# One launch of masked attention and a gated product: the second chunk's attention steps moved to later slots of the first product stage

## The chip, the cores and the metric

The kernel runs as one program on one core of a Trainium2 chip. The metric is the device time of one execution, in microseconds (us); it is the median of several runs. The profile is one more execution of the same program, taken with the hardware profiler. TensorE is called PE below, VectorE DVE, ScalarE ACT, GpSimd POOL, and SyncE, which issues most loads, SP.

## What is computed

Attention over 4 batches, 8 heads, 768 positions, head size 64, in which a query sees the first 4 keys (sinks) and the last 128 keys. Its output is the input of a gated product with weights of 512 x 1536, 512 x 1536 and 1536 x 512:

```python
scores = scale * q @ k.T
scores = np.where(is_sink | in_window, scores, -1e9)
a = np.exp(scores - scores.max(-1, keepdims=True))
x = (a / (a.sum(-1, keepdims=True) + 1e-09)) @ v      # (4*768, 512) after joining the heads
return ((x @ w_a) * (x @ w_b)) @ w_out                # (3072, 512)
```

The weights come to the chip as 64-bit floating numbers, two 32-bit words each, and are made into 32-bit ones there.

## The kernel before

The 3072 rows are worked off in 8 chunks of 2 to 4 blocks of 128 rows. Chunk 0 has 4 blocks (512 rows, batch 0), chunk 1 has 2 (the rest of batch 0). Each chunk has an attention phase, which gives its `xf`, and a product stage, `moe`. While the product stage of chunk c runs, the attention of chunk c+1 is worked in between. The attention of chunk 0 stands alone ahead of everything (`first_attention`, tiles `kp`, `qp`, `p`, `t`, `avp`, `sktp`, `skp`).

**Product stage.** Twelve values of j. For each, `half("a", j)` and `half("b", j)` make 12 matmuls of 512 columns each (L852): each of x and the weight is held as a high part and a remainder (`xh`, `xl`; `wh`, `wl` inside one tile `w`), and of the four products the three larger are added. ACT copies a to `g` (L871), DVE multiplies it by b (L877), ACT rounds it to `gh` (L880), DVE makes the remainder `gl` (L882). Then `project` of the j before multiplies with the third weight into `o`, another 12 matmuls (L861). So one j is 36 matmuls of 512 columns. In chunk 0, PE works this off in the order a, b, o of the j before.

**Weights.** They are made during chunk 0 alone, a pair of two weights at a time: DVE shifts and joins words (L335, L337), ACT scales the low words (L336), DVE adds (L344), ACT rounds to the high part (L349), DVE takes the remainder (L354). `ahead` calls `weights_to` ahead of each third of a j, and pins these instructions to program order. The loads, `raw`, are issued by SP.

**Attention of the next chunk.** The generator `pipeline` is advanced by `between(s)`, called three times in a j, at slots s = 0, 1, 2, ... 35. Its first step is `do_prep` of head 0, which issues the loads of k, q, v (`kr`, `qr`, `v`, `vsr`) and makes high parts (`round`, L381, in chunk 1 on ACT) and remainders (`rest`, L386, in chunk 1 on DVE). Each later step makes the scores of one block of one head (two matmuls `s`, L493), the masking on DVE (L501), exp on ACT (L503), and so on to `p`; two steps later its transposes (`t`, L539), and after every second head a product with v (L434, in chunk 1 into the tile `t`). All this has one PSUM tile for scores and one for the rest in chunk 1. How many steps are to be taken by slot s is the variable `want`.

A scheduler orders the instructions of each engine; it may put an instruction ahead of earlier ones of the program if it is ready, but not those that are given to `keep_in_program_order`, which keep their order among themselves. Every engine works its list off in order. PE's list has each matmul with its weight load (PEld).

The functions that the diff touches, and what calls them:

Of the kernel before, what the change touches and what calls it, by code (L numbers as in the profile page):

```python
# [7 lines left out]
F32 = mybir.dt.float32  # L8
# [5 lines left out]
ALU = mybir.AluOpType  # L14
# [22 lines left out]
SINGLE, PAIRS = 2, 14  # L37
WARM = 8
FILL = {1: 3, 2: 6, 3: 2, 4: 2, 5: 2, 6: 2}
HALF, QUIET, MID = 4, 6, 18  # L40
H_MIN = 1.375 * 2.0 ** -12
H_SUM = 65536.0
I_SIGN = -2147483648
# [14 lines left out]
def verdict(tc, cp, ident, chk, val, gp):  # L58

    nc, pin = tc.nc, tc.keep_in_program_order  # L60
    V = nc.vector
    bad = cp.tile([P, 8], F32, name="bad")
    mm = cp.tile([P, 2], F32, name="mm")
    V.tensor_reduce(mm[:, 0:1], chk[:, :6 * NJ], axis=AX.X, op=ALU.min)
    V.tensor_reduce(mm[:, 1:2], chk[:, 6 * NJ:], axis=AX.X, op=ALU.max)
    pin(V.tensor_scalar(bad[:, 0:1], mm[:, 0:1], H_MIN, None, op0=ALU.is_ge))
    pin(V.tensor_scalar(bad[:, 1:2], mm[:, 1:2], H_SUM, None, op0=ALU.is_lt))
    pin(V.tensor_scalar(bad[:, 2:3], val[:, 0:1], 0.0, None, op0=ALU.is_ge))
    pin(V.tensor_scalar(bad[:, 3:4], val[:, 0:1], float(NS), None, op0=ALU.is_le))
    pin(V.tensor_scalar(bad[:, 4:5], val[:, 1:2], 1.0, None, op0=ALU.is_ge))  # L70
    pin(V.tensor_scalar(bad[:, 5:6], val[:, 1:2], float(P), None, op0=ALU.is_le))
    good = cp.tile([P, 2], F32, name="good")
    V.tensor_reduce(good[:, 0:1], bad[:, 0:6], axis=AX.X, op=ALU.min)
    flag = cp.tile([1, 1], I32, name="flag")
    nc.tensor.transpose(gp, good[:, 0:1], ident)
    V.tensor_reduce(flag, gp, axis=AX.X, op=ALU.min)
    return nc.values_load(flag[0:1, 0:1], min_val=0, max_val=1,
                          skip_runtime_bounds_check_because="a comparison gives 0 or 1")
# [139 lines left out]
class Fast:  # L218
# [159 lines left out]

    def round(self, o, i):
        if self.no_gpsimd:  # L380
            self.nc.scalar.copy(o, i)  # L381
        else:
            self.nc.gpsimd.tensor_scalar(o, i, 1.0, 1.0, op0=ALU.mult, op1=ALU.mult)  # L383

    def rest(self, o, i, high):
        (self.nc.vector if self.no_gpsimd else self.nc.gpsimd).tensor_tensor(o, i, high.bitcast(F32), op=ALU.subtract)  # L386

    def halves(self, h):
        return (slice(0, D), slice(D, P)) if h % 2 == 0 else (slice(D, P), slice(0, D))
# [509 lines left out]
    def run(self, scalars, verdict):  # L899
        chunks = CHUNKS  # L900

        order = self.order = sorted(((k, j) for j in range(NJ) for k in "abo"), key=lambda w: 3 * w[1] + (0, 1, 5)["abo".index(w[0])])
        done, loaded = [0], [0]

        def weights_to(n, ahead):
            wide = range(SINGLE, 2 * PAIRS)
            while loaded[0] < min(n + ahead, len(order)):
                if loaded[0] >= len(order) - 4 and done[0] <= 2 * PAIRS:
                    break
                self.load_weight(loaded[0])  # L910
                loaded[0] += 1
            while done[0] < min(n + DELAY, len(order) + DELAY):
                k = done[0]
                done[0] += 1
                singles = lambda d: 0 <= k - d < len(order) and k - d not in wide
                if singles(3):
                    self.weight_low(k - 3, 1)
                if k % 2 == 0 and k - 2 in wide:
                    self.weight_low(k - 2, 2)
                if singles(2):  # L920
                    self.weight_high(k - 2, 1)
                if singles(1):
                    self.weight_sum(k - 1, 1)
                if k % 2 == 1 and k - 1 in wide:
                    self.weight_sum(k - 1, 2)
                    self.weight_high(k - 1, 2)
                if singles(0):
                    self.weight_bits(k, 1)
                if k % 2 == 0 and k in wide:
                    self.weight_bits(k, 2)  # L930

        light = [c for c in range(2, len(chunks) - 1) if chunks[c + 1][1] == 0]
        checks = [(c, 3 * j) for c in light for j in range(2, 11)]
        checks += [(len(chunks) - 1, 3 * j + i) for j in range(9) for i in range(2)]

        b, t0, nt = chunks[0]

        x = self.wp.tile([P, NK, nt * P], F32, tag=f"w{3 * NJ // 2 - 1}", name="xf0")
        xf = [x[:, i, :] for i in range(NK)]
        first = self.first_attention(b, nt, xf)  # L940
        next(first)
        val = scalars()
        self.masks(val)
        self.val = val
        self.verdict = lambda gp: verdict(val, gp)
        for k, _ in enumerate(first, 1):
            if k >= STEP0 and (k - STEP0) % 3 < 2:
                weights_to(done[0] + 1 - DELAY, 4 + DELAY)
        for c, (b, t0, nt) in enumerate(chunks):
            gen = None  # L950
            if c + 1 < len(chunks):
                nb, nt0, nnt = chunks[c + 1]
                nxf = self.new_xf(c + 1)

                self.banks = ("t", "o2") if nt == 2 else ("t",)
                if c == 1:
                    self.join_masks()
                gen = (self.attention if c else self.attention_in_one_bank)(nb, nt0, nnt, nxf)
                steps = H * nnt + 6
            taken = [0]  # L960

            def between(s):
                if gen is None:
                    return
                if c:
                    want = min(steps, -(-steps * (s + 1) // (3 * NJ - 3)))
                else:
                    n = HALF * nnt + 1
                    want = max(-(-n * (s + 1 - QUIET) // (MID - QUIET)), 1)
                    if s >= MID:  # L970
                        want = min(steps, n - (n - steps) * (s + 1 - MID) // (3 * NJ - 3 - MID))
                while taken[0] < want:
                    next(gen, None)
                    taken[0] += 1

            def ahead(s):
                weights_to(max(s + AHEAD, done[0] + 1 - DELAY), LOADS)
                if (c, s) in checks:
                    self.check_weight(*order[checks.index((c, s))])
                elif self.unchecked:  # L980
                    self.check_weight(None, 0)

            self.moe(b * S + t0 * P, nt, xf, between, ahead, c + 1 == len(chunks), c > 1)
            if gen is not None:
                for _ in gen:
                    pass
                xf = nxf
        return val, self.ok
# [73 lines left out]
```

## Time and profile before

| what | value |
|---|---|
| median of 3 runs | 771.61 us (770.12 to 772.09) |
| the profiled execution's own time | 771.76 us |
| its span from first to last instruction | 770.0 us |
| granted TensorE clock over the span | 0.994 |
| PE busy | 755.8 us (98%) |
| DVE busy | 407.1 us (53%) |
| ACT busy | 417.1 us (54%) |
| POOL busy | 239.9 us (31%) |

The profile's page gives shares over the whole span, and the span cut in 40 slices of 19.25 us, each digit the busy share of its slice in tenths. The attention of chunk 0 fills about the first 38 us, the product stage of chunk 0 runs from 37.95 to 165 us, and seven more product stages follow. A timeline row has start, duration, engine, line, operation and tiles; in brackets the idle time of that engine just before it, and what ended it. Since matmuls overlap, the time from one start to the next, not the duration, is what one costs PE.

### The profile page before, as it was taken

The page shows a single profiled execution, that of the slowest core. Times are in us where ns is not written, and L with a number is a line of the kernel's source. Part 1 is how long each engine was busy: PE and PEld are TensorE (multiplying, and loading weights), DVE is VectorE, ACT ScalarE, POOL GpSimd, SP SyncE. Part 2 cuts the span into 40 slices and gives each one's busy share as a digit, 9 for nine tenths or more (in the row PEclk, how much of TensorE's full clock was granted, in tenths as well). Part 3 has the DMA queues.
Part 4 walks back from the last instruction along what each step waited for, and adds up shares of the span by engine and source line. Part 5 has one row for each costly group of instructions (what it writes and reads, how often), then busy time and mean ns, then how long its engine had stood idle before and what let it go on. Part 6 is the DMA issues. An engine that isn't in the chain of part 4 may idle for free.

```text
span 770.0 us, 13053 instructions
## 1 busy us (share of the span) xinstructions
PE 755.8 (98%) x4335; PEld 659.3 (86%) x4336; DVE 407.1 (53%) x1435; ACT 417.1 (54%) x1252; POOL 239.9 (31%) x305
## 2 busy tenths in 40 slices
PE   9989999999999999999999999999999999999996
PEld 4548777789889998999999999999998999899996
DVE  6997999956644454354433454244543445333221
ACT  5865877746645565365434554355664545434431
POOL 1100000155514544165531544224533544102110
PEclk9989999999999999999999999999999999999999
DMA  8995101231221442311211211113333112015511
GB/s 279 333 381 191 39 15 56 73 125 55 59 72 44 122 143 88 114 36 47 63 56 52 60 42 32 63 54 104 111 107 114 65 51 67 2 51 185 170 47 44
DMA packets 43272, 73.35 MB, mean 95 GB/s; under 512 B 4480, under 2 KB 23744, under 8 KB 43200
## 3 DMA queue, kind: packets, MB, share of 16 engines
q1 hardware_dynamic: 40144, 66.96, 26.9%
q10 hardware_dynamic: 3024, 5.51, 1.9%
q8 instruction: 35, 0.57, 0.3%
q14 instruction: 37, 0.30, 0.1%
q0 software_dynamic: 32, 0.00, 0.0%
HBM read 66.16 MB, written 6.29 MB: 94 GB/s over the span
## 4 chain that ended last, share of the span: by engine, by line
PE 88%; DVE 6%; ACT 3%; DMA 1%; issue 1%; SPq 0%; ACTq 0%; DVEq 0%; POOLq 0%
PE a L852 25%; PE b L852 25%; PE o L861 24%; PE s L493 5%; PE av L434 4%; PE t L533 2%; DVE wf L344 1%; DVE w L354 1%; PE t L539 1%; DMA raw<-in_wa_dram 1%; DVE wf L337 1%; PE avp L434 1%; PE skt L554 1%; ACT p L734 1%; ACT w L349 1%
## 5 line engine op out<-in xcount | busy, mean ns | idle before, releaser
L852 PE MATMUL a<-xh,w 128*128 128x384 f32 (+2 forms) x768 | 218.3, 347 | 1.2 <-DVE w L354 0.7
L852 PE MATMUL b<-xh,w 128*128 128x384 f32 (+2 forms) x768 | 215.6, 344 | 1.6 <-DVE w L354 1.1
L861 PE MATMUL o<-w,gh 128*128 128x512 f32 x576 | 184.2, 400 | 0.0
L852 PEld LDWEIGHTS a<-xh,w 128*128 128x128 f32 x768 | 140.0, 189 | 7.7 <-DVE w L354 1.1
L852 PEld LDWEIGHTS b<-xh,w 128*128 128x128 f32 x768 | 139.9, 189 | 6.8 <-DVE w L354 1.5
L852 PE MATMUL a<-xl,w 128*128 128x384 f32 (+2 forms) x384 | 130.5, 340 | 0.1
L852 PE MATMUL b<-xl,w 128*128 128x384 f32 (+2 forms) x384 | 129.9, 338 | 0.0
L877 DVE TENSOR_TENSOR g<-b,g 128x384 f32<-128x384 f32 (+2 forms) x96 | 53.4, 556 | 143.7 <-PE b L852 127.5
L882 POOL TENSOR_TENSOR gl<-g,gh 128x384 fp32r<-128x384 f32 x60 | 61.0, 1016 | 217.5 <-ACT gh L880 213.3
L861 PEld LDWEIGHTS o<-w,gh 128*128 128x128 f32 x576 | 103.7, 189 | 17.7 <-ACT gh L880 0.5
L861 PE MATMUL o<-w,gl 128*128 128x512 f32 x288 | 113.6, 395 | 0.0
L503 ACT ACTIVATE p<-p,st 128x136 f32<-128x136 f32 (+1 forms) x160 | 67.2, 420 | 63.1 <-DVE st L501 62.4
L880 ACT CAST gh<-g 128x384 fp32r<-128x384 f32 (+2 forms) x96 | 49.3, 514 | 87.5 <-DVE g L877 87.1
L871 ACT COPY g<-a 128x384 f32<-128x384 f32 (+2 forms) x96 | 45.4, 472 | 75.4 <-PE a L852 69.8
L852 PEld LDWEIGHTS a<-xl,w 128*128 128x128 f32 x384 | 72.6, 189 | 3.7 <-DVE xl L834 0.7
L852 PEld LDWEIGHTS b<-xl,w 128*128 128x128 f32 x384 | 72.6, 189 | 1.8
L511 ACT ACTIVATE p<-p,st 128x128 f32<-128x128 f32 x120 | 48.6, 405 | 41.7 <-DVE st L506 40.6
L861 PEld LDWEIGHTS o<-w,gl 128*128 128x128 f32 x288 | 54.1, 188 | 13.2 <-DVE gl L882 1.5
L499 DVE COPY_PREDICATED s<-mg,s 128x128 f32<-128x128 int32 x120 | 35.1, 292 | 54.5 <-PE s L493 54.3
L386 POOL TENSOR_TENSOR ks<-kr,ks 64x400 fp32r<-64x400 f32 (+1 forms) x48 | 57.4, 1196 | 3.8
L505 DVE TENSOR_SCALAR st<-st 128x1 f32<-128x1 f32 x160 | 24.4, 152 | 63.6 <-ACT p L503 63.6
L383 POOL TENSOR_SCALAR qh<-qr 128x384 fp32r<-128x384 f32 x48 | 25.0, 520 | 105.8 <-PE s L493 70.9
(145 smaller groups left out, 1118.5 us busy)
## 6 DMA issues: line engine op xcount, KB each, us to landing
qr<-in_qT_dram SPq DMA_DIRECT2D x48, 192.0 KB, 2.4
raw<-in_wa_dram SPq DMA_DIRECT2D x12, 512.0 KB, 7.0
raw<-in_wb_dram SPq DMA_DIRECT2D x12, 512.0 KB, 7.0
raw<-in_wo_dram SPq DMA_DIRECT2D x12, 512.0 KB, 6.9
chk_a<-in_wa_dram SPq DMA_DIRECT2D x24, 256.0 KB, 3.1
chk_b<-in_wb_dram SPq DMA_DIRECT2D x24, 256.0 KB, 2.9
chk_o<-in_wo_dram SPq DMA_DIRECT2D x24, 256.0 KB, 3.0
out_dram<-os ACTq DMA_DIRECT2D x21, 256.0 KB, 2.2
```

What stands on the lines that cost most here:

```text
L386: (self.nc.vector if self.no_gpsimd else self.nc.gpsimd).tensor_tensor(o, i, high.bitcast(F32), op=ALU.subtract)
L434: self.tc.keep_in_program_order(self.nc.tensor.matmul(ps[e * D:(e + 1) * D, i0:i1, :], lhsT=v[:, e, blk, :], rhs=pt[:, e, sl:sl + i1 - i0, :],
L493: nc.tensor.matmul(ps[:, :w], lhsT=q[:, i * P:(i + 1) * P], rhs=ks[:, c0:c0 + w], start=m == 0, stop=m == 1)
L499: nc.vector.copy_predicated(ps[:, KB:], self.up, ps[:, :P])
L503: nc.scalar.activation(p[:, :w], p[:, :w], AF.Exp, bias=st[:, 0:1], scale=-1.0, accum_out=st[:, 1:2])
L511: nc.scalar.mul(p[:, NS:KB], p[:, NS:KB], st[:, 3:4])
L852: nc.tensor.matmul(ps[:, :n], lhsT=w[:, ksl], rhs=x[:, :n], start=kk == 0 and i == 0, stop=kk == NK - 1 and i == 2)
L861: nc.tensor.matmul(outs[i], lhsT=g[:, sl], rhs=w, start=j == 0 and k == 0, stop=j == NJ - 1 and k == 2)
L871: nc.scalar.copy(g[:, :n], pa[:, :n])
L877: nc.vector.tensor_tensor(g[:, :n], pb[:, :n], g[:, :n], op=ALU.mult)
L880: nc.scalar.copy(gh[:, :n], g[:, :n])
L882: e.tensor_tensor(gl[:, :n], g[:, :n], gh[:, :n].bitcast(F32), op=ALU.subtract)
```

## The change

```diff
-HALF, QUIET, MID = 4, 6, 18
+HALF, QUIET, MID = 4, 5, 18
...
     def round(self, o, i):
         if self.no_gpsimd:
-            self.nc.scalar.copy(o, i)
+            self.tc.keep_in_program_order(self.nc.scalar.copy(o, i))
...
     def rest(self, o, i, high):
-        (self.nc.vector if self.no_gpsimd else self.nc.gpsimd).tensor_tensor(o, i, high.bitcast(F32), op=ALU.subtract)
+        if self.no_gpsimd:
+            self.tc.keep_in_program_order(self.nc.vector.tensor_tensor(o, i, high.bitcast(F32), op=ALU.subtract))
+        else:
+            self.nc.gpsimd.tensor_tensor(o, i, high.bitcast(F32), op=ALU.subtract)
...
                     n = HALF * nnt + 1
-                    want = max(-(-n * (s + 1 - QUIET) // (MID - QUIET)), 1)
+                    want = -(-n * (s + 1 - QUIET) // (MID - QUIET))
```

With `nnt` = 2, n is 9. Before, `want` was 1 in slots 0 to 6, and the steps with scores came from slot 7 on (2 steps by slot 7, 3 by slot 8). Now it is 0 up to slot 4, 1 at slot 5, 2 at slot 6, 3 at slot 7. From slot 18 on the formula is the one of before. `no_gpsimd` holds in chunk 1 alone, so the first product stage is the only one that changes: no instruction is added or taken away there, and from the second stage on the order of every engine is as it was.

In the order of the engines (the rows below; lines after 393 stand three lines lower in the changed kernel), `_4_0_1` in a name stands for first block 4, head 0, tile 1; `a_0`, `b_2`, `g_3` have j as their number; the last number of a name is a buffer's.

PE at the change from the first attention to the product stage, where it works on the last transposes of chunk 0's attention (`t_3`) and its product with v (`avp`). Before:

```order
L852 MATMUL b_0_731<-xh_1_666,w_577 128x512
L852 MATMUL a_0_694<-xl_1_667,w_577 128x512
L852 MATMUL a_0_694<-xh_1_666,w_577 128x512
L753 MATMUL t_3_623<-ident,p_3_0_589 128x128 x2
L753 MATMUL t_3_623<-ident,p_3_1_592 128x128 x2
L852 MATMUL a_0_694<-xh_2_670,w_577 128x512
L852 MATMUL b_0_731<-xl_1_667,w_577 128x512
L852 MATMUL b_0_731<-xh_1_666,w_577 128x512
L852 MATMUL b_0_731<-xh_2_670,w_577 128x512
L434 MATMUL avp_636<-pt,vp_368 64x128 x2
L434 MATMUL avp_636<-pt,vp_368 64x256 x6
```

And now:

```order
L855 MATMUL b_0_713<-xh_1_666,w_577 128x512
L756 MATMUL t_3_623<-ident,p_3_0_589 128x128 x2
L756 MATMUL t_3_623<-ident,p_3_1_592 128x128 x2
L437 MATMUL avp_636<-pt,vp_368 64x128 x2
L437 MATMUL avp_636<-pt,vp_368 64x256 x6
L766 MATMUL sktp_646<-ident,sc_2_553 16x128
L766 MATMUL sktp_646<-ident,sc_3_599 16x128
L855 MATMUL a_0_694<-xl_1_667,w_577 128x512
```

The six matmuls of a_0 and b_0 that stood around the transposes now come behind `avp`, which follows the transposes directly.

PE a little later, up to the last parts of a_0, where two score tiles of chunk 1 (`s_4_0_0`, `s_4_0_1`) stood. Before:

```order
L852 MATMUL b_0_731<-xh_2_670,w_577 128x512
L493 MATMUL s_4_0_0_866<-ks_0_4_713,qh_0_4_714 128x264
L771 MATMUL skp_655<-sctp_649,vsp_370 128x256
L493 MATMUL s_4_0_0_866<-ks_0_4_713,ql_0_4_715 128x264
L852 MATMUL a_0_694<-xh_3_674,w_577 128x512
L852 MATMUL b_0_731<-xh_3_674,w_577 128x512
L493 MATMUL s_4_0_1_896<-ks_0_4_713,qh_0_4_714 128x264
L493 MATMUL s_4_0_1_896<-ks_0_4_713,ql_0_4_715 128x264
L852 MATMUL a_0_694<-xl_3_675,w_577 128x512
```

And now:

```order
L855 MATMUL b_0_713<-xh_1_666,w_577 128x512
L774 MATMUL skp_655<-sctp_649,vsp_370 128x256
L855 MATMUL b_0_713<-xh_2_670,w_577 128x512
L855 MATMUL b_0_713<-xl_2_671,w_577 128x512
L855 MATMUL b_0_713<-xh_2_670,w_577 128x512
L855 MATMUL a_0_694<-xh_3_674,w_577 128x512
L855 MATMUL b_0_713<-xh_3_674,w_577 128x512
L855 MATMUL a_0_694<-xl_3_675,w_577 128x512
```

The four score matmuls are gone from here; they stand in b_3 and behind it now.

DVE from the product of j = 2 on, where it makes the weights. Before:

```order
L354 TENSOR_TENSOR w_757<-wf,w_757 128x1024
L877 TENSOR_TENSOR g_2_833<-b_2_839,g_2_833 128x512
L335 TENSOR_SCALAR wf<-raw_682 128x1024
L337 SCALAR_TENSOR_TENSOR wf<-raw_682,wf 128x1024
L882 TENSOR_TENSOR gl_2_854<-g_2_833,gh_2_853 128x512
L344 ISA wf<-raw_682,wf 128x2048
L386 TENSOR_TENSOR vs_4_4_1141<-vsr_4_4_1139,vs_4_4_1141 64x256
L354 TENSOR_TENSOR w_800<-wf,w_800 128x1024
L335 TENSOR_SCALAR wf<-raw_685 128x1024
```

And now:

```order
L354 TENSOR_TENSOR w_739<-wf,w_739 128x1024
L880 TENSOR_TENSOR g_2_833<-b_2_860,g_2_833 128x512
L335 TENSOR_SCALAR wf<-raw_682 128x1024
L337 SCALAR_TENSOR_TENSOR wf<-raw_682,wf 128x1024
L885 TENSOR_TENSOR gl_2_875<-g_2_833,gh_2_874 128x512
L344 ISA wf<-raw_682,wf 128x2048
L387 TENSOR_TENSOR ks_0_4_800<-kr_0_4_796,ks_0_4_800 64x400
L387 TENSOR_TENSOR ql_0_4_802<-qr_0_4_798,qh_0_4_801 128x256
L387 TENSOR_TENSOR vs_0_4_811<-vsr_0_4_809,vs_0_4_811 64x256
L354 TENSOR_TENSOR w_782<-wf,w_782 128x1024
L504 ISA p_4_0_0_847,st_4_0_0_848<-s_4_0_0_844,mg 128x264
L335 TENSOR_SCALAR wf<-raw_685 128x1024
```

All of head 0's and head 1's remainders, the first two maskings of chunk 1, and head 2's remainders, which stood ahead of `g_2`, now stand behind it. By `g_9` both lists have done the same work. On ACT the roundings move along: `ks_0` is rounded behind the weight's rounding that the last row but one waits for.

## Rows read from the trace of the kernel before

**Rows 1.** The profile's page: busy tenths of DVE in 40 slices

```profile
DVE  6997999956644454354433454244543445333221
```

**Rows 2.** Stretches of the first product stage: busy time (x instructions) of each engine

```profile
core 0: us, PE busy (x) PEld busy (x) DVE busy (x) ACT busy (x) POOL busy (x), PEclk, DMA share, GB/s
39.90:57.00 17.10, 13.89 (x54) 8.53 (x54) 15.99 (x28) 10.99 (x21) 0.38 (x2) 0.80 1.03 393
57.00:70.70 13.70, 13.70 (x60) 11.06 (x59) 10.03 (x19) 9.05 (x16) 0.00 (x0) 1.00 0.77 280
70.70:141.30 70.60, 70.38 (x352) 56.05 (x352) 67.19 (x136) 52.79 (x121) 0.24 (x1) 1.00 0.12 38
```

**Rows 3.** Waits of DVE in 70.7 to 141.3: total us, times, longest

```profile
DVE w L354 <- ACT w L349: 3.0, 6, 1.1
DVE gl L882 <- ACT gh L880: 0.4, 1, 0.4
```

**Rows 4.** Waits of PE in 57 to 165.2

```profile
PE s L493 <- DVE st L501: 0.2, 1, 0.2
```

**Rows 5.** PE's timeline at the change to the product stage

```profile
42.44 0.74 PE L852 MATMUL b<-xh,w 128*128 128x512 f32 x2 [1.08 <-DVE w L354]
...
43.95 1.05 PE L753 MATMUL t<-ident,p 128*128 128x128 f32 x4
...
46.64 1.77 PE L434 MATMUL avp<-pt,vp 128*64 128x128 f32 x16
...
51.24 0.39 PE L493 MATMUL s<-ks,ql 128*128 128x264 f32 x1 [0.85 <-DVE ql L386]
52.10 0.50 PE L852 MATMUL a<-xh,w 128*128 128x512 f32 x1 [0.47 <-ACT xh L833]
```

**Rows 6.** ACT's timeline: the copy behind those transposes

```profile
45.04 0.59 ACT L754 COPY pt<-t 128x512 f32<-128x512 f32 x1 [1.24 <-PE t L753]
```

**Rows 7.** PE alone by stretches: busy, granted clock

```profile
43.30:46.70 3.40, 3.40 (x12) 0.50 1.02 401
46.70:53.60 6.90, 5.48 (x32) 0.99 1.03 406
53.60:57.00 3.40, 3.40 (x9) 0.50 1.05 392
```

**Rows 8.** DVE's timeline at chunk 1's first remainders, maskings and sums

```profile
46.30 0.57 DVE L386 TENSOR_TENSOR ks<-kr,ks 64x400 fp32r<-64x400 f32 x1
46.90 1.23 DVE L337 SCALAR_TENSOR_TENSOR wf<-raw,wf 128x1024 int32<-128x1024 int32 x1
...
51.22 0.42 DVE L386 TENSOR_TENSOR vs<-vsr,vs 64x256 fp32r<-64x256 f32 x1
51.67 0.57 DVE L386 TENSOR_TENSOR ks<-kr,ks 64x400 fp32r<-64x400 f32 x1
52.27 0.43 DVE L501 CUSTOM_DVE_ANT_0 p<-s,mg 128x264 f32<-128x264 f32 x1
...
54.37 0.42 DVE L386 TENSOR_TENSOR ql<-qr,qh 128x256 fp32r<-128x256 f32 x1
54.70 0.69 DVE L335 TENSOR_SCALAR wf<-raw 128x1024 int32<-128x1024 int32 x1
...
58.88 0.15 DVE L505 TENSOR_SCALAR st<-st 128x1 f32<-128x1 f32 x1
```

**Rows 9.** ACT's timeline: roundings of k and q, and of a weight pair

```profile
64.39 0.51 ACT L381 CAST ks<-kr 64x400 fp32r<-64x400 f32 x1
64.80 0.40 ACT L381 CAST qh<-qr 128x256 fp32r<-128x256 f32 x1
...
74.99 1.05 ACT L349 CAST w<-wf 128x1024 fp32r<-128x1024 f32 x1 [2.67 <-DVE wf L344]
```

**Rows 10.** PE's timeline: what two score matmuls cost

```profile
78.42 0.28 PE L493 MATMUL s<-ks,qh 128*128 128x264 f32 x1
...
78.66 0.38 PE L539 MATMUL t<-ident,p 128*128 128x128 f32 x2
```

## The prediction

> **What bounds the kernel now.** I read the page first. PE is busy 98% of the span, DVE 53%, but DVE's digits are 9 from 19 to 154 us, with one 7 between, and 6 and less after [rows 1]: the kernel is bound by PE as a whole, and in the first product stage a second engine is as full as PE. Only that stage is reordered, so I read it by stretches. From 39.9 to 57 us PE is busy 13.9 of 17.1 us at a mean granted clock of 0.80; from 57 to 70.7 it is always busy, while DVE works 10.0 of 13.7 us; from 70.7 (the product of j = 2) to 141.3 us (that of j = 9) PE is busy 70.4 of 70.6 us and DVE 67.2 [rows 2]. So there are two places with something to win or to lose: the first, where PE waits and is slow, and the last, where PE has no idle time and DVE 3.4 us.
>
> What DVE's idle time there consists of is in its waits: 3.0 of 3.4 us, in six places, are the wait of a weight's remainder (L354) for ACT's rounding of the same weight [rows 3]. DVE waits for PE practically nowhere, so it has no lead that PE grants it. PE's longest wait after 57 us is 0.2 us, for DVE's masking [rows 4]. Both engines run neck and neck. At the beginning of the stage PE waits 0.85 us for a remainder `ql` of chunk 1, and 0.47 us for ACT's rounding `xh` of the last quarter of x [rows 5]. And the clock is granted at 0.50, the lower level of 1.2 GHz, in two stretches of 3.4 us, 43.3 to 46.7 and 53.6 to 57.0, both after stretches with waits; PE is busy all through both, and in between it is at 2.4 GHz [rows 7].
>
> **The change, part by part.** No work is added or removed. PE's matmuls are the same, so the time moves only by PE's waits and by its clock.
>
> *First place, the waits.* DVE loses there, in the order of the list, a `ks` remainder, `ql`, `vs`, a second `ks`, a masking and a second `ql`; with them goes PE's wait of 0.85 us for `ql`. The wait of 0.47 us for `xh` hangs on a chain that keeps all its links (`avp`, `sktp`, `sctp`, `skp`, `xf`, `xh`), so I leave it. Something new is late: `avp` now follows the transposes `t_3` directly, and it needs ACT's copy of them. That copy began 1.09 us after the transposes did (43.95 to 45.04) and took 0.59 us [rows 5, 6]; before, six big matmuls filled this time up to 46.64. The transposes themselves last about 0.6 us in PE's sequence, so PE now stands some 1.1 us. The four score matmuls that leave this place (0.24 us a pair, 78.42 to 78.66 [rows 10]) give nothing back here, since the chain to `xh` ends when it ends. Sum: -0.85 + 1.1, about +0.3 us. Bounds: -1.3 (both old waits go, the copy is hidden) and +1.1 (only the new one counts).
>
> *First place, the clock.* A stretch of 3.4 us at half speed in which PE has work all the time costs 1.7 us. The first such stretch follows waits that the change leaves alone (1.08 us for a weight at 42.44 [rows 5] the longest), and I expect it to stay. The second follows the 0.85 and 0.47 us waits and two score matmuls that stood between them; with one wait gone and six matmuls put behind `avp`, PE is fuller there, and I take this stretch as gone: -1.7 us. Bounds: 0 (both stay) and -3.4 (both go).
> The Trainium skill ("TensorE: Matmul & The Clock Gate", section "What's actually happening") says that the throttled state is the default which activity releases, and adds that one and the same kernel shows different numbers of slow matmuls from run to run. By its first half the second stretch goes and the sum below stands; by its second half either kernel can have one stretch more or less in any run, which the one trace here can't show.
>
> *Last place, DVE.* What leaves the time before j = 2 arrives behind it. By the order of DVE that is three `ks` remainders at 0.60 us (46.30 to 46.90), three `ql` at 0.33 to 0.42 (54.37 to 54.70 is the step, 0.42 the duration), a `vs` of 0.45 (51.22 to 51.67), two maskings of up to 0.43 and four small sums of up to 0.15 [rows 8]. That is 1.8 + 1.0 + 0.45 + 0.86 + 0.6 = 4.7 us, some 4.3 where ends overlap, as they do at 54.37. From 57 to 70.7 DVE has 3.7 us of idle time that would have covered them, but the new order no longer puts them there. Between the products of j = 2 and j = 9 DVE then has 67.2 + 4.3 = 71.5 us of work, in a stretch that took 70.6 us, and PE gets 0.5 us more (four score matmuls), 70.9. DVE becomes the longer of the two. How much longer depends on its waits for ACT. If moved work filled all 3.4 us of them, the stretch would grow by 0.9 us, or by nothing, if weights are ready early enough to let DVE trail. If none is filled it is 4.3. And there is a new wait: `ks_0`'s remainder stands right behind L344 of a weight pair, but its rounding is now pinned on ACT behind that pair's rounding. ACT needs 1.05 us for the pair and then about 0.4 us for `ks` [rows 9], so DVE stands up to 1.4 us, where before the rounding was long done. That makes 5.7 us the upper bound. I take half of the old waits as filled: 71.5 + 1.7 = 73.2, or +2.6 us. It appears on PE as waits for a weight's parts, 0.5 to 1 us each, mostly at the first `o` or `a` matmul of a new pair.
>
> *Loads.* SP issues the first k, q, v loads after five weight loads more than before, and the weights' loads so much earlier. The remainders need them 25 us later, so nothing waits; a weight load is earlier by less than 2 us and DVE was not waiting for one after 70.7 us [rows 3]. Nothing either way. What the pinning does is in the sums above; after chunk 1 its branch is not taken.
>
> Sum, against the profiled execution's 771.76 us: 0.3 - 1.7 + 2.6 = +1.2 us, 773.0. The median of the runs stands 0.15 us lower than that execution, so 772.8 us for a median.
>
> **The rivals.**
> *The clock stays low twice (slower).* Mechanism: PE stands 1.1 us for the copy within the first slow stretch, and there are still two waits of half a microsecond before `a_1`; if that is enough to keep or bring back the lower clock around 47 to 57 us, the 1.7 us are not won. For it: the first slow stretch came after waits of that size. Against: the stretch between is fuller by six matmuls. Price: 773.0 + 1.7, 774.5 for a median. It decides from one slow stretch of 3.4 us on: with +2.6 and +0.3 the total passes 0.3%.
> *The beginning wins and DVE catches up (faster).* DVE would use its idle time fully, weights would keep their lead, and the shortage would be 0.9 us; the handoff would win both waits, -1.3 us; one slow stretch goes, -1.7: 771.6 + (-2.1) = 769.5; with both gone 767.8. For it: 3.4 us of idle time are there. Against: six places of that idle time are waits for ACT that any later instruction of DVE's list waits behind.
> *The change doesn't do what it says.* Scores don't start later in time or the weights' chain ignores them, and nothing reaches PE: 771.6. Against it: the score matmuls do leave a_0 and the remainders do leave their place in the list.
>
> **How the numbers follow.** A measurement of this kernel can tell about 0.3% from no change, 2.3 us: faster is below 769.3, slower above 773.9. My forecast, 772.8, has 0.47, with its own range of 770.9 to 775.0 (shortage 0.9 to 4.5 us); a fifth of that lies above 773.9, and nearly nothing below 769.3. The slow clock, 774.5, has 0.33, two thirds of it above 773.9. The faster case, 767.8 to 769.5, has 0.13, two thirds of it below 769.3. The idle change has 0.07. Slower: 0.47 x 0.21 + 0.33 x 0.67 + a little = 0.33. Faster: 0.13 x 0.67 + a little = 0.11. Within: 0.56. The range that holds 8 in 10 reaches into both neighbours: 769.3 to 775.9.
>
> **What would show it.** In the changed kernel's profile: PE's wait for `ql` at the start is gone, and one of about 1 us for ACT's copy stands before `avp`; the granted clock is 0.50 once, not twice, before 60 us; the start of b_1 is earlier than before by 1 to 3 us; DVE is busy 95% and more from j = 2 to j = 9 with a wait of over 1 us before `ks_0`; PE has waits of 0.5 to 1 us for weights there, 2 to 3 us together, and the first matmul of the second stage is later than 165 us by about 1 us. I am wrong if PE shows no such waits after 70 us, or if the stage's end is earlier than before.

## The result, and the profile after

The changed kernel takes 776.07 us (median of 5 runs, 774.41 to 777.11), the kernel before 771.35 in the same comparison. The ratio is 1.0055 with a 95% interval of 1.0041 to 1.0069: slower, by 3.2 to 5.3 us. The forecast was 772.8, the range 769.3 to 775.9, both reckoned from a median of 771.61 before; by the ratio that median becomes 775.9, at the upper end of the range. The profiled execution took 775.94 us, with a span of 774.2.

To see where the time went I cut the first product stage in two at the end of b_2. Times are from first matmul to first or last matmul in PE's timelines; matmul records are complete there.

| | a_0 to the end of b_2 | end of b_2 to the second stage | whole stage |
|---|---|---|---|
| before | 31.87 us | 95.14 us | 127.01 us |
| after | 30.83 us | 100.31 us | 131.15 us |
| difference | -1.0 | +5.2 | +4.1 |

So the beginning won one microsecond, and what followed lost five. In this execution a_0 also began 1.5 us later (39.45 against 37.95). PE's list is the same up to there, and the last section shows that it comes and goes from one execution to the next, with and without the change; so I count from a_0 on. The stages behind the first, whose order has not changed, took 605.1 us before and 603.6 after, and 603.2 to 605.4 in the 14 profiles of this document; so the difference of the two spans, 4.2 us, is 1.5 before a_0, 4.1 in the stage and -1.5 behind it, and only the middle one lies where the order has changed.

The page's DVE digits of the kernel after, beside [rows 1]:

```profile
DVE  6887998976644554344533545334544445433321
```

The slice from 116 to 135 us is 8 where it was 9, and the one from 155 on is 7 where it was 5: DVE was not fuller than before, it stood more and finished later.

The same stretches as in [rows 2], of the kernel after:

```profile
39.90:57.00 17.10, 13.39 (x50) 7.51 (x49) 13.44 (x23) 9.35 (x16) 1.37 (x2) 0.80 1.04 398
57.00:70.70 13.70, 13.70 (x60) 11.06 (x59) 10.02 (x11) 6.39 (x8) 0.00 (x0) 1.00 0.63 251
70.70:141.30 70.60, 68.75 (x330) 51.73 (x331) 64.78 (x132) 51.65 (x120) 0.00 (x0) 1.00 0.12 38
```

In the last one PE does 330 matmuls where it did 352, and DVE is busy 64.8 us where it was 67.2, although 4.3 us of work had been moved in (some of both is the later a_0, since these stretches are counted from the start of the span). DVE's waits there, and PE's from 57 to 165.2 us, after:

```profile
DVE w L354 <- ACT w L349: 2.3, 2, 1.5
DVE g L880 <- PE b L855: 2.0, 2, 1.2
DVE ks L387 <- ACT ks L381: 1.5, 1, 1.5
DVE p L504 <- PE s L496: 0.3, 1, 0.3
```

```profile
PE o L864 <- ACT w L349: 0.5, 1, 0.5
PE o L864 <- DVE w L354: 0.5, 1, 0.5
PE a L855 <- DVE w L354: 0.5, 1, 0.5
PE a L855 <- ACT w L349: 0.2, 1, 0.2
```

Beside [rows 3] and [rows 4]: the longest wait for w, 1.5 us here and 1.1 there, ended at 69.5 us and belongs before this stretch. Without it DVE's waits of 2.3 us have become 4.6, 2.0 of them for PE; and PE waits for weights, which it did not before.

### The profile page after: what moved, and what is told of

Its sections match the earlier page's. It is cut to its first block, busy times and chain, and to the rows that moved or that the text cites. A ratio compares the mean times of both kernels' runs of the same rounds, so it can differ in the third digit from the quotient of the medians.

```text
span 774.2 us, 13057 instructions
## 1 busy us (share of the span) xinstructions
PE 758.7 (98%) x4336; PEld 656.8 (85%) x4336; DVE 408.0 (53%) x1435; ACT 414.8 (54%) x1252; POOL 240.3 (31%) x305
## 4 chain that ended last, share of the span: by engine, by line
PE 92%; DVE 4%; ACT 2%; DMA 1%; issue 1%; SPq 0%; DVEq 0%; ACTq 0%
PE a L855 26%; PE b L855 25%; PE o L864 25%; PE s L496 5%; PE av L437 4%; PE t L536 2%; PE t L542 1%; PE avp L437 1%; DMA raw<-in_wa_dram 1%; ACT p L737 1%; PE skt L557 1%; PE sk L569 1%; PE t L437 1%; DVE xl L837 0%; PE warm L293 0%
```

## How the lost time arises, row by row

DVE's timeline of the kernel after, at the first remainders of chunk 1, and ACT's at the same place (in brackets the idle time just before, and what ended it):

```profile
73.79 1.22 DVE L344 CUSTOM_DVE_ANT_0 wf<-raw,wf 128x2048 uint16<-128x2048 uint16 x1
76.55 0.57 DVE L387 TENSOR_TENSOR ks<-kr,ks 64x400 fp32r<-64x400 f32 x1 [1.54 <-ACT ks L381]
77.15 0.43 DVE L387 TENSOR_TENSOR ql<-qr,qh 128x256 fp32r<-128x256 f32 x1
77.61 0.42 DVE L387 TENSOR_TENSOR vs<-vsr,vs 64x256 fp32r<-64x256 f32 x1
```

```profile
75.04 1.05 ACT L349 CAST w<-wf 128x1024 fp32r<-128x1024 f32 x1 [2.97 <-DVE wf L344]
76.00 0.52 ACT L381 CAST ks<-kr 64x400 fp32r<-64x400 f32 x1
```

DVE ends the weight's sum at 75.01 and comes to ks_0's remainder. ACT had been idle for 2.97 us, but its list had the weight's rounding first (the one that the row of `w_782` waits for in the order shown with the change), and that needed DVE's sum. So DVE waits through the weight's rounding and the one of ks_0. The weight's remainder (L354), ready at 76.1, stands behind three remainders until 78.

A second place is the end of b_5. PE's, ACT's and DVE's timelines, after:

```profile
98.55 0.39 PE L855 MATMUL b<-xh,w 128*128 128x512 f32 x1
99.46 0.97 PE L864 MATMUL o<-w,gh 128*128 128x512 f32 x3 [0.52 <-ACT w L349]
```

```profile
97.64 0.52 ACT L381 CAST ks<-kr 64x400 fp32r<-64x400 f32 x1
98.06 0.41 ACT L381 CAST qh<-qr 128x256 fp32r<-128x256 f32 x1
98.36 1.05 ACT L349 CAST w<-wf 128x1024 fp32r<-128x1024 f32 x1
```

```profile
96.58 1.22 DVE L344 CUSTOM_DVE_ANT_0 wf<-raw,wf 128x2048 uint16<-128x2048 uint16 x1
98.98 0.69 DVE L880 TENSOR_TENSOR g<-b,g 128x512 f32<-128x512 f32 x1 [0.85 <-PE b L855]
99.59 1.22 DVE L354 TENSOR_TENSOR w<-wf,w 128x1024 fp32r<-128x1024 f32 x1
```

The weight's sum was done at 97.8, its rounding began at 98.36 because a ks and a qh stood ahead of it, and PE could not go on until it had ended. DVE's list had g_5 next and the weight's remainder behind it, so DVE waited 0.85 us for the end of b_5. All three engines give time away here, each to another. PE loses more than the bracket says: from 98.55 to 99.46 is 0.91 us, where one such matmul costs 0.23, so 0.68. The same again at 121.13 to 122.04.

## The experiments

The stage column splits as above; the ratio is to the kernel before, timed in the same comparison (5 rounds each).

| run | a_0 to b_2's end | to the second stage | ratio, 95% interval |
|---|---|---|---|
| after | 30.83 | 100.31 | 1.0055 [1.0041, 1.0069] |
| pins alone (e1) | 30.82 | 96.04 | 0.9996 [0.9985, 1.0007] |
| later begin alone (e2) | 32.49 | 94.44 | 1.0003 [0.9992, 1.0013] |
| remainders on POOL (e3) | 30.49 | 101.28 | 1.0060 [1.0045, 1.0076] |
| fill before avp (e4) | 29.29 | 100.29 | 1.0032 [1.0021, 1.0044] |
| preparation early again (e5) | 31.08 | 97.28 | 1.0002 [0.9993, 1.0011] |
| QUIET 6 again (e6) | 30.41 | 97.71 | 1.0013 [1.0004, 1.0022] |
| pins, fill (e7) | 29.28 | 96.22 | 0.9979 [0.9970, 0.9988] |
| pins, eight fills (e8) | 28.40 | 96.06 | 0.9957 [0.9944, 0.9971] |
| head 0's roundings free (e9) | 30.92 | 97.94 | 1.0021 [1.0012, 1.0030] |
| roundings pinned alone (e10) | 30.72 | 99.33 | 1.0039 [1.0023, 1.0055] |
| before, eight fills (e11) | 31.03 | 95.16 | 0.9992 [0.9980, 1.0004] |
| late preparation, no pins, fills (e12) | 28.78 | 95.51 | 0.9960 [0.9945, 0.9975] |

**The parts by themselves.** e1 is the kernel before with the new `round` and `rest`; e2 the kernel before with

```diff
-HALF, QUIET, MID = 4, 6, 18
+HALF, QUIET, MID = 4, 5, 18
...
-                    want = max(-(-n * (s + 1 - QUIET) // (MID - QUIET)), 1)
+                    want = -(-n * (s + 1 - QUIET) // (MID - QUIET))
```

Two theories stood against each other: that DVE is short of time once its work stands behind j = 2, and that the pins themselves hold DVE up.

> Only the pinning of chunk 1's roundings and remainders; the steps begin as in the kernel before. I count the first product stage from the first matmul of a_0 to the first of the second stage: 127.0 us before, 131.2 in the changed kernel. Shortage theory (work of DVE that comes behind the product of j = 2 can't be made up there, weights get late, PE waits for them): only head 0's remainders (0.57 + 0.42 + 0.42 us) stand ahead of j = 2, so the stage is 131.2 - 1.4 = about 129.8 us and the run about 774.5. Pins theory (what costs is that a pinned remainder holds DVE's list up until its pinned rounding has come, whenever the steps begin): as the changed kernel, 776. If neither, 771.4 as before.

> Only the later begin (no step before the sixth slot), without pinning: the scheduler puts heads 0's and 1's remainders and head 0's maskings ahead of the product of j = 1 again. Shortage theory: no work of DVE is moved behind j = 2, so the stage is 127 to 128 us, the run 771.4 to 772.5, and PE has no wait for a weight after 70 us. Pins theory: also 771.4. If the late begin or the late loads cost by themselves, 774 or more.

Neither costs anything that can be measured: 771.57 and 771.80 us. e1 speaks against both theories as I had put them: 1.4 us less of moved work made not 1.4 but 4.3 us of difference, and pins don't cost by themselves. The loss belongs to the parts together. e2 agrees with the shortage theory, but it alone doesn't tell it from the other.

**Work off DVE.** e3 is the changed kernel with

```diff
-            self.tc.keep_in_program_order(self.nc.vector.tensor_tensor(o, i, high.bitcast(F32), op=ALU.subtract))
+            self.tc.keep_in_program_order(self.nc.gpsimd.tensor_tensor(o, i, high.bitcast(F32), op=ALU.subtract))
```

> The changed kernel with chunk 1's remainders on POOL in place of DVE: DVE loses 8 x 0.57 + 8 x 0.41 + 2 x 0.42 = 8.7 us of work, the order of the steps and the pinned roundings stay. Shortage theory: DVE has room from j = 2 on, PE's waits for weights after 70 us (3 us) go, the stage is about 127 us, the run 771 to 772. Pins theory: the pinned roundings still stand before weights' roundings on ACT, so PE still waits, 775 to 776; with POOL's remainders twice as long (1.05 against 0.57 us) scores may come late, and it could be slower still.

775.96 us, nothing won. PE's waits from 57 to 170 us in this run:

```profile
PE s L496 <- POOL ql L387: 2.5, 3, 1.3
PE s L496 <- POOL ks L387: 0.9, 1, 0.9
...
```

The waits for weights are gone, as the shortage theory has it, but 3.4 us of waits for POOL's remainders stand in their place. It shows what a slower engine costs here, and doesn't decide between the theories.

**One condition undone.** e5 is the changed kernel with `max(..., 1)` back, e6 the one with `QUIET` = 6 back.

> The changed kernel with only the floor of one step put back: head 0's loads, roundings and remainders are prepared from slot 0 on again, the scores still begin at the sixth slot, all pinned. Neither part alone cost anything, so it must be what they do together. Late-preparation theory: with the pins nothing of head 0 can be pulled ahead of j = 2, and 4.3 us of DVE's work stand behind it; with head 0's three remainders (1.4 us) back ahead of j = 1 and DVE's idle time of 57 to 70 us used, the stage is 127 us and the run 771 to 772. Rival, early scores: one slot earlier for the scores puts attention ahead of weights' parts on DVE all along j = 3 to 9; then the stage stays 130 to 131 us, the run 775 to 776.

> The changed kernel with only QUIET = 6 again: preparation at the seventh slot, the scores begin one slot later, all pinned. Late-preparation theory: DVE's work is as late or later, so the stage is 131 us or more, the run 776 or more. Early-scores theory: the attention's steps no longer stand ahead of the weights' parts, the stage is 127 to 128 us, the run 771.5 to 773.

Two new theories, late preparation and early scores, each named one of the two conditions as the cause, and both runs are near the kernel before: 771.48 and 771.63 us, the second some 0.1% slower. So neither holds as it stood: taking away either condition takes back three quarters or more of the lost time by the ratios, and a half or somewhat more of it in the second part (97.3 and 97.7 us, against 100.3 after and 95.1 before). What the two have in common in their traces, and not with the kernel after, is that DVE has no wait for ks there. In both, ACT has rounded head 0's parts ahead of that weight pair: ks at 54.88 us in e5 and at 67.39 in e6, where the kernel after has it at 76.00. In e6 the weight's remainder also stands ahead of head 0's remainders in DVE's list. ACT's timeline of e6:

```profile
67.39 0.52 ACT L381 CAST ks<-kr 64x400 fp32r<-64x400 f32 x1
...
73.08 1.05 ACT L349 CAST w<-wf 128x1024 fp32r<-128x1024 f32 x1 [2.00 <-DVE wf L344]
```

DVE's waits from 70.7 to 141.3 us, of e5 and then e6:

```profile
DVE w L354 <- ACT w L349: 3.3, 5, 1.3
DVE p L504 <- PE s L496: 0.3, 1, 0.3
```

```profile
DVE w L354 <- ACT w L349: 1.5, 3, 0.8
DVE p L504 <- PE s L496: 0.4, 1, 0.4
...
```

**The one wait.** So a third theory: head 0's pinned rounding. e9 is the changed kernel with only ks_0, qh_0 and vs_0 free on ACT; e10 has all roundings pinned as after, and `rest` as before.

```diff
-            self.tc.keep_in_program_order(self.nc.scalar.copy(o, i))
+            c = self.nc.scalar.copy(o, i)
+            if self.head > 0:
+                self.tc.keep_in_program_order(c)
...
+        self.head = h
```

> The changed kernel with only head 0's three roundings (ks_0, qh_0, vs_0) not pinned; all else stays. Head-0 theory: ACT then rounds them ahead of the weights' roundings, DVE's wait of 1.54 us for ks_0 goes, and with it what follows from it (in DVE's list the weights' remainders then stand ahead of g_5 and g_7, not behind them, where DVE waited 0.85 and 1.17 us for PE, and PE for the weights). The stage is 128 to 128.5 us as in the two runs that took one of the conditions away, the run 772 to 772.5. Rival, pins in general: 15 of 18 roundings are still pinned and still stand ahead of weights' roundings; then 775 to 776.

> The changed kernel with the remainders on DVE not pinned, the roundings on ACT pinned. Head-0 theory: the pinned rounding of ks_0 still comes behind a weight's on ACT, so DVE still waits over 1 us for it, and free remainders now stand ahead of weights' remainders: stage 131 us or more, 776 or more. Rival (the remainders' pin holds DVE's list up): 771.5 to 772.5.

e9 takes 773.22 us, 2.6 us less than the kernel after by the ratios. That is what the head-0 theory said, a little above its 772.5, and far from the 775 of pins in general: three of 18 roundings hold nearly half of the 5.2 us. DVE's timeline of e9 at the place shown above:

```profile
72.41 1.22 DVE L344 CUSTOM_DVE_ANT_0 wf<-raw,wf 128x2048 uint16<-128x2048 uint16 x1
73.66 0.57 DVE L389 TENSOR_TENSOR ks<-kr,ks 64x400 fp32r<-64x400 f32 x1
74.26 0.43 DVE L389 TENSOR_TENSOR ql<-qr,qh 128x256 fp32r<-128x256 f32 x1
74.72 0.42 DVE L389 TENSOR_TENSOR vs<-vsr,vs 64x256 fp32r<-64x256 f32 x1
75.17 1.23 DVE L354 TENSOR_TENSOR w<-wf,w 128x1024 fp32r<-128x1024 f32 x1
```

ACT's timeline of e9 has ks_0's rounding 24 us ahead of that remainder, so its data had long been there:

```profile
49.24 0.53 ACT L381 CAST ks<-kr 64x400 fp32r<-64x400 f32 x1
```

The three remainders now fill just the time that ACT needs for the weight, and L354 follows without a wait. After that DVE has no wait for PE's b either, and PE none for ACT's rounding. PE's waits from 57 to 165.2 us in e9:

```profile
PE a L858 <- DVE w L354: 0.5, 1, 0.5
PE o L867 <- DVE gl L888: 0.2, 1, 0.2
```

In e10 (774.87 us) the wait of 1.5 us for ks is there again, and its 99.33 us lie near the 100.31 of the kernel after; the time is below the "776 or more" expected, but its interval overlaps that of the kernel after, so whether free remainders help a little stays open. One thing e9 doesn't keep apart: with the rounding free, the scheduler also put the weights' remainders ahead of g_5 and g_7 in DVE's list. The 2.4 us are those of the wait and of this order together.

**The clock.** e4 is the changed kernel, e7 the pins alone, each with three matmuls on zeros (`FZ` = 3) before the last avp; e8 is e7 with two and three matmuls more where a_0 and b_0 wait for their first weights; e11 the kernel before with all eight; e12 the kernel before with all eight and without `max(..., 1)`.

```diff
+            if pr == NP - 1:
+                o = self.ps.tile([P, DM], F32, tag="av", name="fillz")
+                for _ in range(FZ):
+                    self.tc.keep_in_program_order(
+                        nc.tensor.matmul(o, lhsT=self.z[:, :P], rhs=self.z, start=True, stop=True))
             ps = self.ps.tile([P, 4, P], F32, tag="av", name=f"avp{pr}")
...
+GAP = {(0, 'a', 0, 0, 1): 2, (0, 'b', 0, 0, 1): 3}
...
+                    for _ in range(GAP.get((row, kind, j, kk, i), 0)):
+                        nc.tensor.matmul(outs[0], lhsT=w[:, ksl], rhs=x[:, :n], start=True, stop=True)
```

> The changed kernel with three matmuls on zeros (128 x 512, 0.22 us each at the full clock) between the last transposes and avp, where PE waits 0.68 us for ACT's copy. Clock theory (this wait is what keeps the clock at 0.50 for a second stretch): the low stretch ends after 3.4 us in place of 6.8, avp takes 1.8 us in place of 3.25, the run is 1.7 us shorter, 774.4. Otherwise the low stretch stays 6.8 us long and the run is 776, or later by what of the fill doesn't fit the wait.

> The kernel with the pins alone, and the three matmuls on zeros before avp. Its low clock is one stretch of 6.8 us, as in the changed kernel, and it waits 0.68 us for the same copy. Clock theory: the second half of the low stretch goes, 1.7 us, so about 769.9. Otherwise 771.6.

> As the last one, with five more matmuls (0.23 us each) where PE waits 0.52 and 0.71 us for the first weights of a_0 and b_0, two and three; they write into o's tile, which the first real matmul into it clears. If the low clock follows PE's waits just before it, the first stretch goes as well: 1.7 us more, 768.2. If the wait of 1.3 us that is left (b_0 for its weight's remainder) is enough for it, 769.9; later than that by up to 0.5 us if the fills hold a_0 and b_0 up.

> The kernel before with the eight fills (three before avp, two and three at the first weights' waits). Its low clock was two stretches of 3.4 us. If the fills keep the clock up here as they did with the pins, 2 x 1.7 us go: 768.2. In this kernel PE's wait of 0.85 us for ql and the scores among a_0 and b_0 stay, so one stretch may stay: 769.9.

> Best guess: no pins, scores as in the kernel before, but no step before its slot (the floor of one step gone, so head 0's scores leave the first product), and the eight fills. Without pins the scheduler puts head 0's remainders ahead of j = 1, so DVE isn't late; PE's wait for ql goes and the clock stays up. 767 to 767.7, as or below the pins with fills; if the loads that come later cost, 769.

In e4 the first part of the stage is 1.54 us shorter than after, and the second the same; the run 774.56. e7 against e1: again 1.54 us shorter there, 769.18. The timed runs agree: from 1.0055 to 1.0032 and from 0.9996 to 0.9979, some 1.8 and 1.3 us. PE by stretches (busy, granted clock) in the kernel after, then in e4, then in e8:

```profile
43.30:44.94 1.64, 0.77 (x4) 1.00 1.05 377
44.94:51.77 6.83, 6.16 (x27) 0.50 1.04 394
51.77:57.00 5.23, 4.74 (x16) 1.00 1.04 397
```

```profile
44.40:47.81 3.41, 3.41 (x16) 0.50 1.04 401
47.81:57.00 9.19, 8.71 (x42) 1.00 0.91 329
```

```profile
40.00:44.40 4.40, 2.94 (x12) 1.00 1.03 406
44.40:47.81 3.41, 3.39 (x25) 1.00 1.02 417
47.81:57.00 9.19, 8.47 (x33) 1.00 0.99 376
```

With the fill the low stretch is half as long; with all fills there is none, though PE still waits 1.30 us for b_0's weight just before 42.49 us. e8, 767.70 us, and e12, 769.28, are faster than both kernels; by their intervals neither is ahead of the other, though e12 was expected at 767 to 767.7, or at 769 if later loads cost something. The Trainium skill ("TensorE: Matmul & The Clock Gate", section "What's actually happening") says that the throttled state is the default and activity releases it: e8 agrees, useless matmuls kept the clock at its upper level. In the kernel before the same fills win nothing that can be measured (e11, 772.09 us, 0.9992), where 768.2 to 769.9 was expected. In the profiled execution the first part of the stage is 0.8 us shorter, but PE's wait of 0.8 us for `ql` stayed there, and a low stretch behind it, of e11:

```profile
40.00:54.40 14.40, 11.56 (x56) 1.00 1.00 381
54.40:57.81 3.41, 3.41 (x8) 0.50 1.05 389
```

So the new handoff from the first attention to the product stage is worth having, if it is filled.

## Why the prediction was right in places and wrong in size

**The waits at the handoff.** Foreseen and there: `ql`'s wait is gone, and one for ACT's copy stands before avp, 0.68 us in the bracket and 0.89 from start to start (1.10 from the last transpose at 45.18 to avp, where the step before was 0.21), for the 1.1 forecast. (Of the six matmuls that the prediction puts into this time, four stood behind the transposes before; two stood ahead of them.) PE's timeline of the kernel after, beside [rows 5], and ACT's copy, beside [rows 6]:

```profile
44.17 0.73 PE L855 MATMUL b<-xh,w 128*128 128x512 f32 x2 [1.31 <-DVE w L354]
44.75 0.86 PE L756 MATMUL t<-ident,p 128*128 128x128 f32 x4
46.28 3.25 PE L437 MATMUL avp<-pt,vp 128*64 128x128 f32 x16 [0.68 <-ACT pt L757]
54.31 0.50 PE L855 MATMUL a<-xh,w 128*128 128x512 f32 x1 [0.28 <-ACT xh L836]
```

```profile
45.64 0.59 ACT L757 COPY pt<-t 128x512 f32<-128x512 f32 x1 [1.04 <-PE t L756]
```

The wait for `xh` that I left alone shrank from 0.47 to 0.28. Waits and clock together I had at 0.3 - 1.7 = -1.4 us; the first part of the stage became 1.0 us shorter.

**The clock.** This term was wrong. The low clock lasts 6.83 us in both kernels: two stretches of 3.41 in [rows 7], one of twice that here. The rival that the clock stays low had it, with its mechanism: PE stands for the copy within the low stretch, and avp runs at half speed, 3.25 us in place of the 1.77 of [rows 5]. e4 and e7 show that this wait is what keeps it, and that half of it is worth 1.5 us. That the first part won 1.0 us all the same must lie with the waits and with the four score matmuls that left it, where I had +0.3 and nothing. So it is luck that -1.0 came near the -1.4: the clock gave none of its 1.7 us, and the rest, forecast as a loss, won. The rows divide the 1.0 us at the end of the wait for `xh`. It came 14.15 us after a_0 before (52.10) and 14.86 after (54.31), 0.7 us later although `ql`'s wait had gone; the whole of the low clock now lies ahead of it, where half of it did before. Behind it, 17.7 us became 16.0: there the second low stretch of before and two of the score matmuls had stood. No run keeps the score matmuls and the waits apart.

**DVE's shortage.** The direction was right, the size wrong: +2.6 forecast, +5.2 measured between the end of b_2 and the second stage. The shape was right as well: PE's waits are for weights, at `o` and `a`. e9 divides the size: 100.31 - 97.94 = 2.4 us are the wait for ks_0's pinned rounding and what follows from it. The 2.8 us that e9 leaves (97.94 - 95.14) lie near what the sum had for the work moved behind j = 2, but that they are this work is not shown: in e9 15 roundings and all remainders are still pinned, and no run keeps these apart from it. In e1, where head 0's remainders stand ahead of j = 2 and the scores begin a slot later, only 96.04 - 95.14 = 0.9 us are left. I had named the wait for ks_0, at up to 1.4 us (it was 1.54), but put it only into the upper bound of 5.7 and not into the value. The step that failed is "I take half of the old waits as filled: 71.5 + 1.7 = 73.2, or +2.6 us", with the new wait at nothing. I had also written that DVE would be 95% busy from j = 2 to j = 9. It was 64.78 of 70.60 us, 92%: a wait on a pinned list doesn't fill an engine, it empties it. One reading was off, too: of the 3.0 us of waits for weights that the prediction took from [rows 3], the longest, 1.1 us, ended at 69.53 and lies ahead of the stretch, so 1.9 of DVE's 3.4 us of idle time there were such waits.

**What the sum left out altogether.** PE, ACT and DVE wait for one another in a ring. I had taken DVE's lateness as something that PE sees and pays once. In the rows at 98 us DVE also waits for PE, 2.0 us in two places, and ACT's pinned roundings come between.

**Loads.** No wait of DVE or PE for a load after 57 us; nothing either way, as forecast.

**The signs named.** b_1 began 1.0 us earlier, counted from a_0; the low clock came once, as named, but for twice as long; the second stage began at 170.6 us in place of about 166, 1.5 of it from before a_0.

Sum for the stage: -1.0 + 2.8 + 2.4 = +4.2. These are differences out of one table, so they must add up to the +4.1 measured there but for rounding; the timed runs, 3.2 to 5.3, stand apart from it and agree.

## What to carry to other kernels

Where two engines hand work back and forth, ask for each instruction that is pinned on one of them what stands ahead of its partner on the other: a wait at the head of a list costs its own length and then comes back as waits of the others. When two parts of a change cost nothing by themselves, that is no evidence for the two together; run them undone one by one from the full change as well. A price named for a bound belongs into the sum, if the order of the lists already shows that it will be paid.

## What was not expected of the hardware

The granted clock of the rows missed a low stretch at the start of one execution here. PE's matmuls on zeros (128 x 512) in the first attention, of the kernel after and then of the one before:

```profile
7.11 1.46 PE L726 MATMUL fill<-z 128*128 128x512 bf16 x3
```

```profile
6.28 0.82 PE L723 MATMUL fill<-z 128*128 128x512 bf16 x3
```

The records behind these rows start 0.40 to 0.43 us apart in the one and 0.22 to 0.23 in the other, at the same granted clock of 1.00 in the rows for 6.20 to 9.10. In e4 three such matmuls started 0.43 us apart at 45.55 us, where the rows grant 0.50. The Trainium skill ("TensorE: Matmul & The Clock Gate", section "Wait — 56ns, not 53.3ns?") has 426.7 ns from start to start for such a matmul at 1.2 GHz and 215.7 at 2.4, which is what these two show: the kernel after began at the lower level, and a_0 came 1.5 us later for it. In e4, e7 and e11 a recorded low stretch of 3.41 us at 34 us put a_0 at 39.5 to 39.6 as well; in the other nine experiments, and in the kernel before, it was at 37.8 to 38.0, pins and late begin among them. The first attention was thus some 1.5 us longer or shorter from one execution to the next, and a comparison of two profiles has to begin behind it.
